# Small operations of a spectral block and gated MLP regrouped and moved between engines, on one core

## The chip, the core and the metric

The kernel runs on one core of a Trainium2 chip. A core has five engines that run side by side, each through its own list of instructions in order: TensorE (PE in the profile; PEld is its weight load) multiplies matrices, VectorE (DVE) and ScalarE (ACT) work element by element and read what TensorE leaves in PSUM, GpSimd (POOL) works element by element on SBUF, and SyncE (SP) issues the transfers between HBM and SBUF. An instruction waits on semaphores until what it reads is there, and everything behind it on its engine waits with it. The metric is the device time of one execution in microseconds (us), lower is better.

## What is computed

One token row set `x` of 8192 x 448 goes through two residual branches. `c` (448 numbers) gives six rows of 448 by `silu(c) @ w_mod`: shift, scale and gate of each branch.

```python
mod = (_silu(c) @ w_mod).reshape(c.shape[0], 6, 1, -1)
sa, ca, ga, sb, cb, gb = (mod[:, i] for i in range(6))
h = _layernorm(x) * (1 + ca) + sa
x = x + ga * irfft2(softshrink(block_mlp(rfft2(h))))      # 4 blocks of 112, complex, two layers
h = _layernorm(x) * (1 + cb) + sb
x = x + gb * ((gelu(h @ w_gate) * (h @ w_up)) @ w_down)   # 448 -> 1792 -> 448
```

The spelling of the spectral line is shortened here; the transform runs over the 8192 rows, the two layers of the MLP use complex 112 x 112 weights, and the shrink is by 0.01. All inputs and the output are float32.

## The kernel before

The program has three stages, written out engine by engine in the order of the source (`manual_schedule`), so the order of the source is the order of every engine's list.

**Stage one** (lines 130 to 330) reads `x` as 64 slices of 128 x 448 (`bb`, loaded four at a time as chunks `ch`), takes the mean and variance of each row, and multiplies each slice by the first Fourier factor `f1`, scaled by the rows' inverse deviation. A group of slices goes through a chain: VectorE takes statistics (`stats`, line 161) and joins them (`aggr_steps`), ScalarE takes a square root (line 188), VectorE makes the inverse and one correction step of Newton's method (lines 189 to 193, into `y`) and the scaled mean `nm`; then for each slice a scaled copy `fr` of `f1` is made (line 204 on ScalarE, line 206 on GpSimd), TensorE multiplies (`dft_a`, line 211), and ScalarE copies the result out of PSUM with the mean taken off (`out_a`, line 216). `means` (line 183) is one small matmul for each group. `store_t` writes finished chunks to `td` in HBM. The groups are `cuts` = 0, 2, 4, 8, 16, 24, 40, 56, 60, 64; a small planner (`ex`, `run`, with rough times `dve` and `pe`) sorts the calls and so interleaves the chain of one group with the statistics of the next. At its end two modulation rows (`mod_row0`, `mod_turn`, `mod_cols`) become columns.

**Stage two** works through 32 units. `step(i)` (line 534) issues, in this order: the loads of unit i + 2 (`fetch_t`), the hooks "load" and "pe", `stage_s2` of unit i, `split_t` of unit i + 1 (its low half `tl` on GpSimd), the hook "act", `stage_m2` of unit i - 2 with the split of its result (`yl` on GpSimd, twice), `stage_i1` of unit i - 3, the hook "dve", `stage_m1` of unit i - 1. The hooks, filled by `at(i, hook, ...)`, carry preparation for stage three: loads and norms of the gate and up weights (`load_w`, `squares`, `norms`: steps 1 to 16), sums of the down weights (`down_sums`), and the modulation rows. `load_mod_row` loads 4 x 112 rows of `w_mod`, and `mod_row` makes one modulation row on all partitions with 16 weight-and-matmul passes (8 matmuls of 128 x 224, line 637). Small operations on scales are put into a list `tiny` (by `VL` and `GL`, which record an operation for VectorE or GpSimd) and issued one by one between the larger ones by `drip()`. `all_max` (line 680) takes a maximum over partitions: TensorE turns a column (`turn`), VectorE reduces it, and TensorE spreads it again (`spread`) into the same PSUM bank of tag "pd", which `stage_i1` also uses; a tag has two banks.

**Stage three** (line 900 on) is the second branch: gate, up and down products over 32 row groups of 256.

Of the kernel before, what the change touches and what calls it, by code (L numbers as in the profile page):

```python
# [10 lines left out]
F32 = mybir.dt.float32  # L11
# [34 lines left out]
def spectral_geglu(ctx, tc, x, wt_in, wgu, wd, cvec, wmod, cf1, cs2, cmi, cgm, out):  # L46
# [88 lines left out]
    with ExitStack() as actx:  # L135
# [41 lines left out]
        def scale_steps(bs):  # L177

            g = slice(bs[0], bs[-1] + 1)

            def means():
                ps = bank("pc", "psmu")
                T.matmul(ps[:, : len(bs)], f1, nm[:, g], start=True, stop=True)
                S.copy(mu[:, g], ps[:, : len(bs)])


            return [
                lambda: S.activation(q[:, g], mv[:, g, 1], AF.Sqrt, bias=eps),
                lambda: V.reciprocal(q[:, g], q[:, g]),
                lambda: V.tensor_tensor(t[:, g], q[:, g], q[:, g], ALU.mult),  # L190
                lambda: V.scalar_tensor_tensor(t[:, g], mv[:, g, 1], EPS, t[:, g], op0=ALU.add, op1=ALU.mult),
                lambda: V.scalar_tensor_tensor(t[:, g], t[:, g], -0.5, q[:, g], op0=ALU.mult, op1=ALU.mult),
                lambda: V.scalar_tensor_tensor(y[:, g], q[:, g], 1.5, t[:, g], op0=ALU.mult, op1=ALU.add),
                lambda: V.scalar_tensor_tensor(nm[:, g], mv[:, g, 0], -0.5 if len(bs) >= 8 else -1.0, y[:, g], op0=ALU.mult, op1=ALU.mult),
                means,
            ]
# [3 lines left out]
        def scaled(bb):  # L200

            f = ap.tile([128, 128], F32, tag="fr", name="fr", bufs=6)
            if bb < 8 or bb % 4 == 3:
                S.activation(f, f1, AF.Copy, scale=y[:, bb : bb + 1])
            else:
                G.tensor_scalar(f, f1, y[:, bb : bb + 1], None, op0=ALU.mult)
            frs[bb] = f
# [82 lines left out]
        for g, bs in enumerate(groups + [[]]):  # L290
            done = None
            if pend:
                aggr, sqrt, rest, mean = pend
                run(aggr)
                ex(dve, sqrt)
                ready = dve + 0.6
            for bb in bs:
                if pend and not done and dve >= ready:
                    run(rest)
                    done = dve  # L300
                ex(dve, stats, bb)
# [32 lines left out]
    with ExitStack() as bctx:  # L334
# [260 lines left out]
        for z in zh + hh_:  # L595
            V.tensor_copy(z[96:113, 0], ones[96:113])
        mod_turn()
        mod_cols()
        split_t(*units[0], el=V)
        bp = bctx.enter_context(tc.tile_pool(name="bp", bufs=1, side="right"))  # L600
# [21 lines left out]
        def load_mod_row(pool, q):  # L622
            out = []
            for hh in range(2):
                if pool is None:
                    wm = bp1.tile([128, GB, HC], F32, tag="tr", name="tr", bufs=2)[:112]
                else:
                    wm = raw_tile(pool)[:112, :, :HC]
                dma(wm, wmod[q][:, :, hh * HC : (hh + 1) * HC])
                out.append(wm)  # L630
            return out

        def mod_row(key, dst=None):
            ps = bank("pd", "psm")
            for hh, wm in enumerate(raws.pop(key)):
                for k in range(4):
                    T.matmul(ps[:, hh * HC : (hh + 1) * HC], cs[:, k : k + 1].to_broadcast([112, 128]), wm[:, k, :], start=k == 0, stop=k == 3)
            if dst is None:
                return ps[:, :D]
            S.copy(dst, ps[:, :D])  # L640

        def row_scales():

            VL.tensor_scalar(cb_r, cb_r, 1.0, None, op0=ALU.add)
# [3 lines left out]
            VL.scalar_tensor_tensor(bnd, rmax[:, 0:1], 21.2, rmax[:, 1:2], op0=ALU.mult, op1=ALU.add)  # L648
            VL.tensor_scalar(bnd, bnd, 1.01, 1e-30, op0=ALU.mult, op1=ALU.add)
            pow2(sk, bnd)  # L650
            VL.tensor_scalar(sb_r, sb_r, sk, None, op0=ALU.mult)
            VL.tensor_scalar(cb_r, cb_r, sk, None, op0=ALU.mult)

# [25 lines left out]
        def all_max(dst, src, n, first=(), then=()):  # L679
# [12 lines left out]
            def spread():  # L692
                T.matmul(at_[0][:, 128 : 128 + n], onesr[:n], dia, start=True, stop=True)

            VL.tensor_copy(col, src)
            tiny.extend(first or [free] * 3)
            tiny.append(turn)
            tiny.append(lambda: V.tensor_reduce(top, at_[0][:n, :128], mybir.AxisListType.X, ALU.max))
            VL.tensor_scalar(dia, identb[:n, :n], top, None, op0=ALU.mult)
            tiny.extend(then or [free] * 3)  # L700
            tiny.append(spread)
            tiny.append(lambda: V.tensor_copy(dst, at_[0][:, 128 : 128 + n]))

# [4 lines left out]
        def scales1():  # L708
# [9 lines left out]
            first = [  # L718
                lambda: V.tensor_tensor(hb2, rmax[:, 0:1], rmax[:, 1:2], ALU.add),
                lambda: V.tensor_tensor(hb2, hb2, hb2, ALU.mult),  # L720
                lambda: V.tensor_scalar(hb2, hb2, 1.02 * D, 1e-30, op0=ALU.mult, op1=ALU.add),
            ]

            then = [
                lambda: V.tensor_tensor(mx2, nrm[:, 0], nrm[:, 1], ALU.mult),
                lambda: V.tensor_scalar(mx2, mx2, hb2, None, op0=ALU.mult),
                lambda: V.tensor_tensor(sa_act, mx2[:, :NP], mx2[:, NP:], ALU.max),
# [3 lines left out]
        def scales2():  # L731
            pow2(sw, mxa)
            inv_pow2(dsw, sw)
            inv_pow2(hs, sk)
            VL.tensor_scalar(dsw, dsw, hs, None, op0=ALU.mult)
            VL.tensor_copy(dg, dsw[:, 0:1])
            pow2(sa_act, sa_act, 13)
            inv_pow2(isa, sa_act)
            VL.tensor_scalar(sa_act, sa_act, dsw[:, 1:2], None, op0=ALU.mult)

        def down_scales():

            VL.tensor_tensor(dsc, dn, isa, ALU.mult)
            VL.tensor_reduce(hs, dsc, mybir.AxisListType.X, ALU.max)
# [155 lines left out]
    with ExitStack() as cctx:  # L900
# [417 lines left out]
```

## Time and profile before

| what | value |
| --- | --- |
| time, median of 3 runs (lowest to highest) | 1981.11 us (1980.15 to 1984.56) |
| the profiled execution: its time, its span | 1981.5 us, 1979.7 us |
| mean granted TensorE clock | 0.99 |
| VectorE, ScalarE, GpSimd busy | 58%, 39%, 60% of the span |
| stage one; stage two; stage three | about 0 to 84; 84 to 410; 410 to 1980 us |

The page lists busy times by engine; the timeline of one engine gives start, duration, line, operation, output <- inputs, and in brackets how long the engine was idle before and what released it. A float32 matmul counts as two or more passes, so a count such as x4 stands for two matmuls of 448 columns. The windows view gives, for each stretch, the busy time of PE, PEld, DVE, ACT and POOL with their counts, the mean granted TensorE clock, the busy share of the transfer engines and GB/s.

### The profile page before, as it was taken

The page shows a single profiled execution, that of the slowest core. Times are in us where ns is not written, and L with a number is a line of the kernel's source. Part 1 is how long each engine was busy: PE and PEld are TensorE (multiplying, and loading weights), DVE is VectorE, ACT ScalarE, POOL GpSimd, SP SyncE. Part 2 cuts the span into 40 slices and gives each one's busy share as a digit, 9 for nine tenths or more (in the row PEclk, how much of TensorE's full clock was granted, in tenths as well). Part 3 has the DMA queues.
Part 4 walks back from the last instruction along what each step waited for, and adds up shares of the span by engine and source line. Part 5 has one row for each costly group of instructions (what it writes and reads, how often), then busy time and mean ns, then how long its engine had stood idle before and what let it go on. Part 6 is the DMA issues. An engine that isn't in the chain of part 4 may idle for free.

```text
span 1979.7 us, 43432 instructions
## 1 busy us (share of the span) xinstructions
PE 1922.4 (97%) x17674; PEld 1710.8 (86%) x17674; DVE 1141.2 (58%) x2355; ACT 767.7 (39%) x1290; POOL 1184.7 (60%) x1479
## 2 busy tenths in 40 slices
PE   6899989988999999999999999999999999999998
PEld 3598989977888888888888888889888888989898
DVE  7478889866555554555555555555555555555533
ACT  5665658643333333333333333333333333333322
POOL 2355646536666666666666666666666666666644
PEclk9899989999999999999999999999999999999999
DMA  9797757641111111111111111111111111111000
GB/s 347 265 284 248 228 147 221 169 149 45 56 43 43 45 49 46 43 42 43 43 42 45 49 42 43 43 42 42 43 43 43 43 43 44 43 42 44 22 16 20
DMA packets 150539, 165.75 MB, mean 84 GB/s; under 512 B 83953, under 2 KB 125169, under 8 KB 149954
## 3 DMA queue, kind: packets, MB, share of 16 engines
q1 hardware_dynamic: 150338, 162.97, 27.2%
q8 instruction: 138, 2.26, 0.5%
q14 instruction: 63, 0.52, 0.1%
HBM read 97.49 MB, written 49.66 MB: 74 GB/s over the span
## 4 chain that ended last, share of the span: by engine, by line
PE 85%; DVE 10%; ACT 3%; issue 1%; DMA 1%; POOL 1%; SPq 0%; ACTq 0%; DVEq 0%; POOLq 0%
PE pgu L1033 52%; PE pdn L1101 7%; PE pdn L1099 7%; PE pdn L1100 7%; DVE y L469 3%; PE ps L211 2%; DVE zl L384 1%; DVE t L461 1%; DVE hl L439 1%; PE pi L933 1%; DVE st L161 1%; PE pi L931 1%; PE pi L932 1%; PE ps L375 0%; DVE wd L868 0%
## 5 line engine op out<-in xcount | busy, mean ns | idle before, releaser
L1033 PE MATMUL pgu<-nt,wh 128*128 128x256 f16 x6272 | 833.0, 273 | 1.8 <-DVE nt L1024 1.8
L1033 PEld LDWEIGHTS <-wh 128*128 128x128 f16 x6272 | 601.9, 98 | 99.2 <-issue 32.2
L1069 ACT ACTIVATE gel<-pgu,dg 128x256 f32<-128x256 f32 x448 | 200.4, 473 | 797.8 <-PE pgu L1033 762.8
L1033 PE MATMUL pgu<-nt,wl 128*128 128x256 f16 (+1 forms) x3584 | 500.7, 272 | 0.0
L1099 PE MATMUL pdn<-wd,ac 128*128 128x224 f16 x1568 | 407.0, 260 | 2.0 <-ACT p L1128 2.0
L1101 PE MATMUL pdn<-wd,ac 128*128 128x224 f16 x1568 | 406.9, 260 | 0.2 <-DVE ac L1092 0.2
L1100 PE MATMUL pdn<-wd,ac 128*128 128x224 f16 x1568 | 406.9, 260 | 0.0
L1080 POOL TENSOR_TENSOR x<-x 128x128 f32<-128x128 f32 x223 | 242.3, 1087 | 234.2 <-DVE x L1074 234.2
L1092 DVE SCALAR_TENSOR_TENSOR ac<-x,sa_act,ac 128x896 f16<-128x896 f32 (+1 forms) x225 | 308.2, 1370 | 83.6 <-ACT ac L1091 83.6
L1033 PEld LDWEIGHTS <-wl 128*128 128x128 f16 (+1 forms) x3584 | 297.6, 97 | 56.6 <-issue 23.6
L1074 DVE TENSOR_TENSOR x<-pgu,gel 128x256 f32<-128x256 f32 x448 | 179.6, 418 | 284.4 <-ACT gel L1069 283.7
L1091 ACT ACTIVATE ac<-x,sa_act 128x896 f16<-128x896 f32 (+1 forms) x225 | 232.9, 1035 | 48.8 <-POOL x L1083 46.7
L1134 POOL TENSOR_TENSOR o<-u,p 128x224 f32<-128x224 f32 x32 | 21.1, 658 | 294.3 <-DVE u L1133 294.3
L1081 POOL TENSOR_TENSOR x<-x 128x128 f32<-128x128 f32 x223 | 159.9, 717 | 17.5
L1100 PEld LDWEIGHTS <-ac 128*128 128x128 f16 x1568 | 153.8, 98 | 2.7 <-issue 2.1
L1099 PEld LDWEIGHTS <-ac 128*128 128x128 f16 x1568 | 153.7, 98 | 0.8 <-issue 0.2
L1101 PEld LDWEIGHTS <-ac 128*128 128x128 f16 x1568 | 153.7, 98 | 0.7 <-DVE ac L1092 0.5
L106 POOL TENSOR_TENSOR yl<-y,yh 128x448 fp32r<-128x448 f32 x63 | 77.8, 1235 | 90.9 <-ACT yh L104 82.9
L1082 POOL TENSOR_TENSOR x<-x 128x128 f32<-128x128 f32 x223 | 114.7, 515 | 0.0
L1083 POOL TENSOR_TENSOR x<-x 128x128 f32<-128x128 f32 x223 | 107.6, 482 | 0.0
L469 DVE TENSOR_TENSOR y<-pm,t 64x224 f32<-64x224 f32 x256 | 99.5, 389 | 8.2
L106 POOL TENSOR_TENSOR tl<-tr,th 128x896 f16<-128x896 f32 x30 | 57.4, 1914 | 67.6 <-ACT th L104 64.8
(288 smaller groups left out, 2794.9 us busy)
## 6 DMA issues: line engine op xcount, KB each, us to landing
tr<-td SPq DMA_DIRECT2D x64, 224.0 KB, 4.3
raw<-in_gu SPq DMA_DIRECT2D x28, 512.0 KB, 5.9
vd<-us SPq DMA_DIRECT2D x64, 224.0 KB, 3.0
xx<-in_x SPq DMA_DIRECT2D x32, 448.0 KB, 3.2
v<-vd SPq DMA_DIRECT2D x64, 224.0 KB, 2.7
out<-x SPq DMA_DIRECT2D x31, 448.0 KB, 2.6
nt<-pk SPq DMA_TRANSPOSE x480, 2.3
tb<-in_x SPq DMA_DIRECT2D x8, 896.0 KB, 17.5
```

The source lines that it names most:

```text
L106: (el or V).tensor_tensor(lo, src, h, ALU.subtract)
L469: V.tensor_tensor(y[ri * 64 : ri * 64 + 64, gi], pv[si, ri], tv[si, ri], ALU.subtract)
L1033: T.matmul(pgu[i, t, q][:, pr * H : (pr + 1) * H], w[rows, tw, f0 : f0 + 128], nts[i][rows, tn, :], start=start, stop=stop, skip_group_che ...
L1069: S.activation(gl, ps[:, :H], AF.Gelu_apprx_tanh, scale=dg)
L1074: V.tensor_tensor(dst, ps[:, H : 2 * H].rearrange("p (b c) -> p b c", b=2), gl.rearrange("p (b c) -> p b c", b=2), ALU.mult)
L1080: e.tensor_tensor(s1, a21, a22, ALU.add)
L1081: e.tensor_tensor(s2, s1, a11, ALU.subtract)
L1091: S.activation(ac[:, 0, k], x[:, k], AF.Copy, scale=sc)
L1092: V.scalar_tensor_tensor(ac[:, 1, k], x[:, k], sc, ac[:, 0, k], op0=ALU.mult, op1=ALU.subtract)
L1099: T.matmul(ps, ac[:, 0, ka], wds[t][:, 0, kb], start=t == 0, stop=False)
L1100: T.matmul(ps, ac[:, 0, ka], wds[t][:, 1, kb], start=False, stop=False)
L1101: T.matmul(ps, ac[:, 1, ka], wds[t][:, 0, kb], start=False, stop=t == NP - 1)
```

## The change

1. Stage one: groups of at most eight slices, the Newton step written with one operation less, and the scaled copies `fr` of slices 0 to 3 on VectorE and of 4 to 7 on GpSimd instead of ScalarE. The planner waits for two statistics (`ready`), not one, between square root and inverse in the later groups.
2. Modulation rows: all four rows of stage three are loaded in stage two (steps 1, 3, 5, 8). GpSimd multiplies the four tiles of a row by the columns of `cs` and adds them up in place (`mod_sum`, one step later, hook "dve"), and TensorE sums the 112 partitions with one matmul by ones (`mod_row`, at the head of the step after that, hook "pe").
3. `row_scales` moves from step 9 to step 6, and many small operations of the scales move from VectorE to GpSimd.
4. `all_max` takes a bank for `turn` and another for `spread`.
5. `gb_r` is scaled on GpSimd in step 24, and the first `split_t` stands ahead of `mod_turn`.

```diff
-        cuts = [0, 2, 4, 8, 16, 24, 40, 56, 60, 64]
+        cuts = [0, 2, 4, 8, 16, 24, 32, 40, 48, 56, 60, 64]
...
-                lambda: V.tensor_tensor(t[:, g], q[:, g], q[:, g], ALU.mult),
-                lambda: V.scalar_tensor_tensor(t[:, g], mv[:, g, 1], EPS, t[:, g], op0=ALU.add, op1=ALU.mult),
+                lambda: V.scalar_tensor_tensor(t[:, g], mv[:, g, 1], EPS, q[:, g], op0=ALU.add, op1=ALU.mult),
...
-            if bb < 8 or bb % 4 == 3:
+            if bb >= 8 and bb % 4 == 3:
                 S.activation(f, f1, AF.Copy, scale=y[:, bb : bb + 1])
             else:
-                G.tensor_scalar(f, f1, y[:, bb : bb + 1], None, op0=ALU.mult)
+                (V if bb < 4 else G).tensor_scalar(f, f1, y[:, bb : bb + 1], None, op0=ALU.mult)
...
-                ready = dve + 0.6
+                ready = dve + (0.6 if g < 3 else 1.2)
...
+        def mod_sum(key):
+            r = raws[key]
+            G.tensor_scalar(r[0], r[0], cs[:, 0:1], None, op0=ALU.mult)
+            for k in range(1, 4):
+                G.tensor_scalar(r[k], r[k], cs[:, k : k + 1], None, op0=ALU.mult)
+                G.tensor_tensor(r[0], r[0], r[k], ALU.add)
+
+        def mod_row(key, dst):
             ps = bank("pd", "psm")
-            for hh, wm in enumerate(raws.pop(key)):
-                for k in range(4):
-                    T.matmul(ps[:, hh * HC : (hh + 1) * HC], cs[:, k : k + 1].to_broadcast([112, 128]), wm[:, k, :], start=k == 0, stop=k == 3)
+            T.matmul(ps[:, :D], onec.to_broadcast([112, 128]), raws.pop(key)[0], start=True, stop=True)
             S.copy(dst, ps[:, :D])
...
             def spread():
-                T.matmul(at_[0][:, 128 : 128 + n], onesr[:n], dia, start=True, stop=True)
+                at_[1] = bank("pd", "pmx")
+                T.matmul(at_[1][:, :n], onesr[:n], dia, start=True, stop=True)
...
-            VL.tensor_scalar(dia, identb[:n, :n], top, None, op0=ALU.mult)
+            GL.tensor_scalar(dia, identb[:n, :n], top, None, op0=ALU.mult)
...
-        at(3, "load", pre, npool, "cb", load_mod_row, 4)
-        at(5, "load", pre, npool, "sb", load_mod_row, 3)
-        at(6, "pe", mod_row, "cb", cb_r)
-        at(8, "pe", mod_row, "sb", sb_r)
+        for n, (key, q, dst) in zip((1, 3, 5, 8), (("cb", 4, cb_r), ("sb", 3, sb_r), ("ga", 2, ga_r), ("gb", 5, gb_r))):
+            at(n, "load", pre, npool, key, load_mod_row, q)
+            at(n + 1, "dve", mod_sum, key)
+            at(n + 2, "pe", mod_row, key, dst)
...
-        at(9, "dve", row_scales)
+        at(6, "dve", row_scales)
...
-        at(31, "load", pre, None, "ga", load_mod_row, 2)
-        at(32, "load", pre, fp, "gb", load_mod_row, 5)
+        at(24, "dve", lambda: G.tensor_scalar(gb_r, gb_r, ds_d, None, op0=ALU.mult))
...
-        mod_row("ga", ga_r)
...
-        gb = mod_row("gb")
...
-        S.copy(gb_r, gb)
...
-        V.tensor_scalar(gb_r, gb_r, ds_d, None, op0=ALU.mult)
```

Where the order of instructions changes, at three places. First GpSimd's list in steps 1 to 3 of stage two (`tl` and `yl` are low halves of float32 values, `raw` the tiles of the row "cb"). Before:

```order
L106 TENSOR_TENSOR tl_929<-tr_814,th_928 128x896
L106 TENSOR_TENSOR yl_955<-y_949,yh_954 128x448
L106 TENSOR_TENSOR yl_979<-y_973,yh_978 128x448
L106 TENSOR_TENSOR tl_1067<-tr_890,th_1066 128x896
L106 TENSOR_TENSOR yl_1093<-y_1087,yh_1092 128x448
```

And of the changed kernel:

```order
L108 TENSOR_TENSOR tl_954<-tr_835,th_953 128x896
L108 TENSOR_TENSOR yl_980<-y_974,yh_979 128x448
L108 TENSOR_TENSOR yl_1004<-y_998,yh_1003 128x448
L633 TENSOR_SCALAR raw_839<-raw_839,cs_79 112x448
L635 TENSOR_SCALAR raw_839<-raw_839,cs_79 112x448
L636 TENSOR_TENSOR raw_839<-raw_839 112x448
L635 TENSOR_SCALAR raw_841<-raw_841,cs_79 112x448
L636 TENSOR_TENSOR raw_839<-raw_839,raw_841 112x448
L635 TENSOR_SCALAR raw_841<-raw_841,cs_79 112x448
L636 TENSOR_TENSOR raw_839<-raw_839,raw_841 112x448
L108 TENSOR_TENSOR tl_1102<-tr_915,th_1101 128x896
```

Seven operations, four products by a column and three additions, now stand between the second `yl` of step 2 and the `tl` of step 3.

Second TensorE's list where step 3 begins (`pm1` is the last matmul of step 2, `pw` the norms). Before:

```order
L425 MATMUL pm1_998<-zl_849,w1h_93 112x256
L426 MATMUL pm1_998<-zh3_735,w1l_94 112x256
L670 LDWEIGHTS sq_932
L670 MATMUL pw_1024<-onesb_73,sq_932 128x1
L670 MATMUL pw_1024<-onesb_73,sq_932 128x1
```

And of the changed kernel:

```order
L426 MATMUL pm1_1030<-zl_874,w1h_95 112x256
L427 MATMUL pm1_1030<-zh3_756,w1l_96 112x256
L640 MATMUL psm_1056<-raw_839,onec_80 128x448
L672 LDWEIGHTS sq_957
L672 MATMUL pw_1059<-onesb_73,sq_957 128x1
```

The matmul that reads the sum `raw_839` is the first of step 3; the same is found at the heads of steps 5, 7 and 10, and the eight matmuls of 128 x 224 for each row, which stood at the heads of steps 6 and 8 and twice between stages two and three, are gone.

Third VectorE's list of stage one around slice 24. Before, a chain of sixteen:

```order
L161 BN_STATS st_132<-xt_129 128x6 x3
L161 BN_STATS st_132<-xt_130 128x6 x4
L161 BN_STATS st_132<-tb 128x6 x8
L170 TENSOR_TENSOR t<-st_132 128x16
L171 TENSOR_TENSOR mv<-st_132 128x16
L189 RECIPROCAL q<-q 128x16
```

And of the changed kernel, two chains of eight:

```order
L163 BN_STATS st_134<-xt_131 128x6 x2
L163 BN_STATS st_134<-xt_132 128x6 x4
L172 TENSOR_TENSOR t<-st_134 128x8
L173 TENSOR_TENSOR mv<-st_134 128x8
L163 BN_STATS st_134<-tb 128x6 x2
L191 RECIPROCAL q<-q 128x8
L163 BN_STATS st_134<-tb 128x6 x6
```

The inverse for slices 24 to 31 now comes after two statistics of the next eight, not after those of sixteen slices.

More of the change, by code (lines that the diff above doesn't have):

```diff
@@ L75, in spectral_geglu @@
     cs = cpool.tile([112, 4], F32, name="cs")
+    onec = cpool.tile([112, 1], F32, name="onec")
+    V.memset(onec, 1.0)
     nrm = cpool.tile([128, 2, NFT], F32, name="nrm")
@@ L189, in scale_steps @@
                 lambda: V.reciprocal(q[:, g], q[:, g]),
-                lambda: V.tensor_tensor(t[:, g], q[:, g], q[:, g], ALU.mult),
-                lambda: V.scalar_tensor_tensor(t[:, g], mv[:, g, 1], EPS, t[:, g], op0=ALU.add, op1=ALU.mult),
+                lambda: V.scalar_tensor_tensor(t[:, g], mv[:, g, 1], EPS, q[:, g], op0=ALU.add, op1=ALU.mult),
                 lambda: V.scalar_tensor_tensor(t[:, g], t[:, g], -0.5, q[:, g], op0=ALU.mult, op1=ALU.mult),
-                lambda: V.scalar_tensor_tensor(y[:, g], q[:, g], 1.5, t[:, g], op0=ALU.mult, op1=ALU.add),
+                lambda: V.scalar_tensor_tensor(y[:, g], t[:, g], 1.5, q[:, g], op0=ALU.add, op1=ALU.mult),
                 lambda: V.scalar_tensor_tensor(nm[:, g], mv[:, g, 0], -0.5 if len(bs) >= 8 else -1.0, y[:, g], op0=ALU.mult, op1=ALU.mult),
@@ L596, in spectral_geglu @@
             V.tensor_copy(z[96:113, 0], ones[96:113])
+        split_t(*units[0], el=V)
         mod_turn()
         mod_cols()
-        split_t(*units[0], el=V)
         bp = bctx.enter_context(tc.tile_pool(name="bp", bufs=1, side="right"))
@@ L623, in load_mod_row @@
             out = []
[L624 to L630, printed above, removed]
-            return out
-        def mod_row(key, dst=None):
-            ps = bank("pd", "psm")
-            for hh, wm in enumerate(raws.pop(key)):
-                for k in range(4):
-                    T.matmul(ps[:, hh * HC : (hh + 1) * HC], cs[:, k : k + 1].to_broadcast([112, 128]), wm[:, k, :], start=k == 0, stop=k == 3)
-            if dst is None:
-                return ps[:, :D]
+            for i in range(2):
+                wm = raw_tile(pool).rearrange("p q c -> p (q c)")[:112, : 2 * D].rearrange("p (q c) -> p q c", q=2)
+                dma(wm, wmod[q][:, 2 * i : 2 * i + 2])
+                out += [wm[:, 0], wm[:, 1]]
+            return out
+        def mod_sum(key):
[5 more added lines that the diff above has]
+        def mod_row(key, dst):
+            ps = bank("pd", "psm")
+            T.matmul(ps[:, :D], onec.to_broadcast([112, 128]), raws.pop(key)[0], start=True, stop=True)
             S.copy(dst, ps[:, :D])
         def row_scales():
-            VL.tensor_scalar(cb_r, cb_r, 1.0, None, op0=ALU.add)
+            GL.tensor_scalar(cb_r, cb_r, 1.0, None, op0=ALU.add)
             for j, r in enumerate((cb_r, sb_r)):
@@ L647, in row_scales @@
             bnd = cpool.tile([128, 1], F32, name="hb")
-            VL.scalar_tensor_tensor(bnd, rmax[:, 0:1], 21.2, rmax[:, 1:2], op0=ALU.mult, op1=ALU.add)
-            VL.tensor_scalar(bnd, bnd, 1.01, 1e-30, op0=ALU.mult, op1=ALU.add)
+            GL.tensor_scalar(bnd, rmax[:, 0:1], 21.2, None, op0=ALU.mult)
+            GL.tensor_tensor(bnd, bnd, rmax[:, 1:2], ALU.add)
+            GL.tensor_scalar(bnd, bnd, 1.01, 1e-30, op0=ALU.mult, op1=ALU.add)
             pow2(sk, bnd)
-            VL.tensor_scalar(sb_r, sb_r, sk, None, op0=ALU.mult)
-            VL.tensor_scalar(cb_r, cb_r, sk, None, op0=ALU.mult)
+            GL.tensor_scalar(sb_r, sb_r, sk, None, op0=ALU.mult)
+            GL.tensor_scalar(cb_r, cb_r, sk, None, op0=ALU.mult)
         def load_w(pool, pr, j):
@@ L692, in spread @@
             def spread():
-                T.matmul(at_[0][:, 128 : 128 + n], onesr[:n], dia, start=True, stop=True)
-            VL.tensor_copy(col, src)
+                at_[1] = bank("pd", "pmx")
+                T.matmul(at_[1][:, :n], onesr[:n], dia, start=True, stop=True)
+            GL.tensor_copy(col, src)
             tiny.extend(first or [free] * 3)
@@ L698, in all_max @@
             tiny.append(lambda: V.tensor_reduce(top, at_[0][:n, :128], mybir.AxisListType.X, ALU.max))
-            VL.tensor_scalar(dia, identb[:n, :n], top, None, op0=ALU.mult)
+            GL.tensor_scalar(dia, identb[:n, :n], top, None, op0=ALU.mult)
             tiny.extend(then or [free] * 3)
             tiny.append(spread)
-            tiny.append(lambda: V.tensor_copy(dst, at_[0][:, 128 : 128 + n]))
+            tiny.append(lambda: V.tensor_copy(dst, at_[1][:, :n]))
         mxa = cpool.tile([128, 2], F32, name="mxa")
@@ L718, in scales1 @@
             first = [
-                lambda: V.tensor_tensor(hb2, rmax[:, 0:1], rmax[:, 1:2], ALU.add),
-                lambda: V.tensor_tensor(hb2, hb2, hb2, ALU.mult),
-                lambda: V.tensor_scalar(hb2, hb2, 1.02 * D, 1e-30, op0=ALU.mult, op1=ALU.add),
+                lambda: G.tensor_tensor(hb2, rmax[:, 0:1], rmax[:, 1:2], ALU.add),
+                lambda: G.tensor_tensor(hb2, hb2, hb2, ALU.mult),
+                lambda: G.tensor_scalar(hb2, hb2, 1.02 * D, 1e-30, op0=ALU.mult, op1=ALU.add),
             ]
             then = [
-                lambda: V.tensor_tensor(mx2, nrm[:, 0], nrm[:, 1], ALU.mult),
-                lambda: V.tensor_scalar(mx2, mx2, hb2, None, op0=ALU.mult),
+                lambda: G.tensor_tensor(mx2, nrm[:, 0], nrm[:, 1], ALU.mult),
+                lambda: G.tensor_scalar(mx2, mx2, hb2, None, op0=ALU.mult),
                 lambda: V.tensor_tensor(sa_act, mx2[:, :NP], mx2[:, NP:], ALU.max),
@@ L734, in scales2 @@
             inv_pow2(hs, sk)
-            VL.tensor_scalar(dsw, dsw, hs, None, op0=ALU.mult)
-            VL.tensor_copy(dg, dsw[:, 0:1])
+            GL.tensor_scalar(dsw, dsw, hs, None, op0=ALU.mult)
+            GL.tensor_copy(dg, dsw[:, 0:1])
             pow2(sa_act, sa_act, 13)
             inv_pow2(isa, sa_act)
-            VL.tensor_scalar(sa_act, sa_act, dsw[:, 1:2], None, op0=ALU.mult)
+            GL.tensor_scalar(sa_act, sa_act, dsw[:, 1:2], None, op0=ALU.mult)
         def down_scales():
-            VL.tensor_tensor(dsc, dn, isa, ALU.mult)
+            GL.tensor_tensor(dsc, dn, isa, ALU.mult)
             VL.tensor_reduce(hs, dsc, mybir.AxisListType.X, ALU.max)
@@ L750, in down_scales2 @@
             pow2(hs, ds_d, 13)
-            VL.tensor_scalar(dsc, isa, hs, None, op0=ALU.mult)
+            GL.tensor_scalar(dsc, isa, hs, None, op0=ALU.mult)
             inv_pow2(ds_d, hs)
```

## The prediction

> **What bounds the kernel now.** I read the engines' shares first, then the busy time by stretches (start:end, length, then busy and count of PE, PEld, DVE, ACT, POOL; granted clock, DMA share, GB/s), then the rows in order of time.
>
> ```profile
> PE 1922.4 (97%) x17674; PEld 1710.8 (86%) x17674; DVE 1141.2 (58%) x2355; ACT 767.7 (39%) x1290; POOL 1184.7 (60%) x1479
> 65.00:68.00 3.00, 3.00 (x9) 1.51 (x9) 2.97 (x8) 2.62 (x6) 3.00 (x3) 1.00 1.01 423
> 104.20:113.30 9.10, 9.03 (x88) 8.60 (x86) 7.47 (x17) 6.06 (x11) 4.30 (x4) 1.00 0.82 240
> 122.10:130.80 8.70, 8.70 (x88) 8.53 (x87) 7.50 (x16) 6.06 (x11) 4.21 (x3) 1.00 1.01 279
> 174.40:187.80 13.40, 10.69 (x99) 9.69 (x98) 13.04 (x31) 7.47 (x16) 5.50 (x5) 1.00 0.61 187
> 242.70:260.10 17.40, 12.00 (x80) 10.81 (x80) 13.02 (x28) 6.64 (x12) 6.05 (x5) 0.80 0.48 129
> 277.20:291.00 13.80, 10.79 (x82) 9.71 (x80) 10.71 (x23) 7.69 (x13) 8.61 (x6) 0.88 0.63 168
> 291.00:299.30 8.30, 8.30 (x80) 8.18 (x80) 6.85 (x18) 6.41 (x10) 3.08 (x2) 1.00 0.39 109
> ```
>
> TensorE is the bound. Row three is step 3 of stage two and row four step 5: PE full, GpSimd half idle. The places where PE isn't full are step 10 (174.40), step 17 (242.70) and step 20 (277.20), where VectorE's list of small scale operations is late, and gaps in stage one. The change touches all of these. My sums are made on the profiled execution, 1981.5 us (its span 1979.7 and 1.8 around it); the median of the runs shown, 1981.11, is the same within 0.4 us.
>
> **The sums on GpSimd.** PE takes its list in order, and the matmul that reads the sum of a row is now the first of steps 3, 5, 7 and 10, ahead of the norms `pw`. GpSimd can begin the seven operations only after the second `yl` of the step before, and these end late:
>
> ```profile
> 104.20 0.60 PE L670 MATMUL pw<-onesb,sq 128*128 128x1 bf16 x8
> 105.42 1.14 POOL L106 TENSOR_TENSOR yl<-y,yh 128x448 fp32r<-128x448 f32 x1 [1.13 <-ACT yh L104]
> 122.08 0.60 PE L670 MATMUL pw<-onesb,sq 128*128 128x1 bf16 x8
> 122.28 1.14 POOL L106 TENSOR_TENSOR yl<-y,yh 128x448 fp32r<-128x448 f32 x1 [1.20 <-ACT yh L104]
> 142.61 0.60 PE L670 MATMUL pw<-onesb,sq 128*128 128x1 bf16 x8
> 142.81 1.14 POOL L106 TENSOR_TENSOR yl<-y,yh 128x448 fp32r<-128x448 f32 x1 [1.20 <-ACT yh L104]
> 173.00 0.60 PE L670 MATMUL pw<-onesb,sq 128*128 128x1 bf16 x8
> 174.13 1.14 POOL L106 TENSOR_TENSOR yl<-y,yh 128x448 fp32r<-128x448 f32 x1 [1.21 <-ACT yh L104]
> ```
>
> When PE arrives at step 3 (104.20), that `yl` still has until 106.56: 2.36 us. The other three pairs give 1.34, 1.34 and 2.27; together 7.3. Then come four products by a column and three additions, each on the result of the one before or two before:
>
> ```profile
> 24.66 3.52 POOL L206 TENSOR_SCALAR fr<-f,y 128x128 f32<-128x128 f32 x6 [22.75 <-DMA tb<-in_x]
> L1113 POOL TENSOR_TENSOR o<-o,gb_r 128x448 f32<-128x448 f32 x62 | 70.3, 1133 | 2.4
> 132.14 0.66 POOL L783 TENSOR_TENSOR m<-m 128x224 f32<-128x224 f32 x1
> 132.88 0.66 POOL L784 TENSOR_TENSOR m<-m 128x224 f32<-128x224 f32 x1
> ```
>
> An addition of 448 columns costs 1.1 us (1133 ns). Dependent ones start 0.74 apart for 0.66 of work, so 0.08 per hand-over, about 0.45 for six. The trace has no product by a column over 448 columns on GpSimd; it has one over 128, at 3.52/6 = 0.59. It cannot be less than 0.59, and 3.5 times that, 2.05, if all of it grows with length. Between them I take 1.4: the `m` and `o` additions grow by 0.47 for 224 more columns, so 0.59 grows by 0.67 for 320 more to 1.26 at their rate, and a little more since the product was slower than an addition to begin with. One sum is then 4 x 1.4 + 3 x 1.1 + 0.45 = 9.3 us (6.1 to 12.0). While it runs everything behind the matmul waits: the norms, the tokens' spectra, the mixing; and ScalarE and VectorE wait for those. PE had no free time in these steps, so the wait is lost: 7.3 + 4 x 9.3 = **+44.5** (31.7 to 55.3).
>
> After a wait the clock is low. The row at 41.69 below shows it: four matmuls took 3.30 after an idle of 3.62, and 1.77 at 25.32. That is 1.55 after a short idle; step 17 had a mean clock of 0.80 over 17.4 us, which is up to 3.5 lost. Four times 2.0: **+8** (6 to 14).
>
> The matmuls themselves:
>
> ```profile
> 130.82 3.19 PE L637 MATMUL psm<-raw,cs 112*128 112x224 f32 x16
> 405.69 3.19 PE L637 MATMUL psm<-tr,cs 112*128 112x224 f32 x16
> 410.12 0.66 ACT L104 CAST vh<-v 128x224 fp32r<-128x224 f32 x2 [0.67 <-DMA vd<-us]
> 414.92 5.92 PE L637 MATMUL psm<-raw,cs 112*128 112x224 f32 x16
> 421.46 0.56 PE L1015 MATMUL ptr<-ident,pk 128*128 128x128 f16 x7 [0.57 <-ACT pk L988]
> ```
>
> Sixteen pieces (0.19 each) held PE 3.0 us in steps 6 and 8. A row of 448 columns is now four pieces, 0.76. The rows "ga" and "gb" stood at 405.69 and 414.92, where PE would have waited anyway: for the transfer behind `vh` (410.12) and for ScalarE's `pk` (421.46). So 4 x 0.76 - 2 x 3.0 = **-3**. With "gb" gone, PE is idle for some 6 us ahead of 421.46 and starts stage three cold: **+2** (0 to 3).
>
> **Stage one.**
>
> ```profile
> 21.20 1.75 PE L211 MATMUL ps<-xt,fr 128*128 128x448 f32 x4
> 23.14 0.31 ACT L188 ACTIVATE q<-mv,eps 128x8 f32<-128x8 f32 x1
> 24.60 3.77 DVE L161 BATCH_NORM_STATS2 st<-xt 128x6 f32<-128x448 f32 x7
> 25.32 1.77 PE L211 MATMUL ps<-xt,fr 128*128 128x448 f32 x4 [2.37 <-POOL fr L206]
> 30.63 3.78 DVE L161 BATCH_NORM_STATS2 st<-xt 128x6 f32<-128x448 f32 x7
> 41.69 3.30 PE L211 MATMUL ps<-xt,fr 128*128 128x448 f32 x4 [3.62 <-POOL fr L206]
> 57.21 12.27 PE L211 MATMUL ps<-tb,fr 128*128 128x448 f32 x32
> 74.37 6.17 PE L228 MATMUL psm<-wm,cs 112*1 112x448 f32 x16
> ```
>
> A slice costs PE 0.757 (the second group spans 30.63 - 24.60 = 6.03 on VectorE). With groups of eight PE has 8 x 0.757 + 0.14 = 6.2 per group and VectorE 6.0, minus 0.2 for the operation dropped, 5.8: the next `fr` are ready before PE wants them, and the idle of 3.62 with its cold 1.55 at 41.69 goes. The start at 25.32 comes about 0.8 sooner, at 24.5: then 56 x 0.757 + 7 x 0.14 = 43.4 ends at 67.9, where stage one ended at 74.37: **-6.4** (-7 to 0, if a chain is late in each group). What is late next is the input: the DMA share is 1.01 until 68, and three stores of 0.22 MB go behind it, some 1.6 us, so 1 or 2 us of the gain may go there.
>
> **The scales and the rest.** Step 17 took 17.4 us and step 20 13.8, while step 21 (291.00) took 8.3.
>
> ```profile
> PE pi L498 <- ACT us L501: 2.3, 1, 2.3
> PE pi L498 <- ACT us L501: 1.9, 1, 1.9
> 178.54 1.11 DVE L514 SCALAR_TENSOR_TENSOR hb<-rmax 128x1 f32<-128x1 f32 x1
> 177.72 1.91 POOL L106 TENSOR_TENSOR tl<-tr,th 128x896 f16<-128x896 f32 x1 [2.46 <-ACT th L104]
> 248.94 1.65 DVE L514 TENSOR_SCALAR mxd<-identb,mxt 2x2 bf16<-2x2 bf16 x1
> ```
>
> Of their 14.6 surplus, PE's wait for the shared bank (first row: step 17; second row: step 20; us, times, longest) goes with the two banks. Small VectorE operations that took 1.1 to 1.65 while GpSimd worked go to GpSimd itself; the reductions stay and still queue. I take a bit more than half: **-8** (-3 to -14.6). `row_scales` moves from step 9 to step 6, behind a wait of PE: the surplus of step 10, 13.4 - 10.7 = 2.7 of PE idle, goes: **-2.7** (0 to -4).
>
> At nothing: the `memset`; the same bytes of "ga" and "gb" loaded 25 steps earlier (PE and not a queue ends those steps; if it did not, 1.6 MB would cost 4 us at 423 GB/s); `split_t` ahead of `mod_turn` (VectorE and PE wait there for `cs` anyway; else its operation, 1.9 by the `tl` row of the same size); the product `gb_r` by `ds_d` on GpSimd in step 24 (idle half of a step; else 1.4). Sum: 44.5 + 8 - 3 + 2 - 6.4 - 8 - 2.7 = +34.4, of 1981.5: **2015 us**, slower.
>
> [...]
>
> **The rivals.** *Cheap sums.* The product costs 0.6 for 448 columns as for 128: a sum is 4 x 0.6 + 3.3 + 0.45 = 6.1, the four 12.8 less: 2002. For it: 0.59 may be mostly a fixed cost. Against: the additions grow with length. *Dear sums.* 2.05 each: 10.6 more, 2026. *Stage one stays broken.* A group of eight waits for its chain as one of sixteen did; 6.4 more: 2022. For it: each hand-over between VectorE, ScalarE and GpSimd costs a fraction of a us and there are more of them now.
> *The wait is absorbed: faster.* In steps 3 to 9 PE's rows look full, but DMA shares are 0.82 and 1.01; if the transfers set the pace, matmuls that look busy are only spread out, a pause at a step's head is caught up later in it, and only the gains are left: 1981.5 - 3 + 2 - 6.4 - 8 - 2.7 = 1963. It decides only if a sum and its `yl` (1.3 to 2.4) fit in what a step can give back; to break even, with gains of 18.1, each wait may cost 18.1/4 = 4.5 in all, so a sum may take 2.7. Three additions alone take 3.3, and the clock in these rows is 1.00 with weight loads at 8.5 of 8.7, so I give it little.
>
> **How the numbers follow.** Forecast 0.50 (2008 to 2022), cheap sums 0.18, dear sums 0.14, stage one broken 0.09, absorbed 0.06, partly absorbed so that nothing can be told 0.03. A measurement of this kernel can tell about 0.2%, 4 us. Faster 0.06, same 0.03, slower 0.91. The range takes in the cheap sums with full gains in the scales (2002 - 6.6, and 5 more from the lower ends of clock and stage one: 1990) and the dear ones with small gains (2026 + 5 and the higher clock cost, 6, and 3 left over: 2040).
>
> **What would show it.** Four idle gaps of PE of 10 to 12 us ahead of `psm`, ended by GpSimd's `raw` in steps 3, 5, 7 and 10, and a lower clock behind each; products on GpSimd near 1.4 us; matmuls without a gap from 25 to 68; steps 17 and 20 nearer to 10 than to 15. It is wrong if PE's gaps there are under 5 us, if the matmul's operand is ready before PE comes, or if the steps with a gap are no longer in all than before.

## The result and the profile after

The changed kernel takes 2015.9 us (2014.7 to 2016.9), the kernel before 1981.0: 1.0172 times as long, 95% interval 1.0155 to 1.0190, or 35 us more. The runs below give this ratio and, in brackets, its interval in the same way. The profiled execution has a span of 2013.8, 34.1 more than the 1979.7 of before.

First the shares of the engines in the profile after; then TensorE's four largest waits, from its rows in order of time (start, us, engine, line, operation; in brackets how long it had waited and for whom).

```profile
PE 1914.2 (95%) x17622; PEld 1700.3 (84%) x17622; DVE 1136.5 (56%) x2351; ACT 764.7 (38%) x1286; POOL 1232.5 (61%) x1532
```

```profile
111.17 1.11 PE L640 MATMUL psm<-raw,onec 112*128 112x448 f32 x1 [11.38 <-POOL raw L636]
143.12 1.11 PE L640 MATMUL psm<-raw,onec 112*128 112x448 f32 x1 [10.40 <-POOL raw L636]
174.49 1.11 PE L640 MATMUL psm<-raw,onec 112*128 112x448 f32 x1 [10.40 <-POOL raw L636]
216.42 1.11 PE L640 MATMUL psm<-raw,onec 112*128 112x448 f32 x1 [11.32 <-POOL raw L636]
```

TensorE has 8 us less work and the kernel is 34 us longer: PE's share falls from 97% to 95%. The four waits, one for each row of the modulation, sum to 43.5 us, at the heads of steps 3, 5, 7 and 10. What ends them are GpSimd's operations on the tile `raw`, shown by the view of that tile (line, operation, count: shortest/median/longest ns, first and last start):

```profile
L635 POOL TENSOR_SCALAR raw<-raw,cs x12: 1404/1406/1409, 103.3 to 213.8; 112x448 f32<-112x448 f32 x12
L636 POOL TENSOR_TENSOR raw<-raw x12: 1127/1127/1127, 104.8 to 215.2; 112x448 f32<-112x448 f32 x12
L633 POOL TENSOR_SCALAR raw<-raw,cs x4: 1405/1407/1411, 101.9 to 207.2; 112x448 f32<-112x448 f32 x4
```

A product of a tile by a column takes 1.41 us, an addition of two tiles 1.13. The busy time by stretches (columns as before) shows the wait of step 3 and what follows it:

```profile
99.50:110.90 11.40, 0.29 (x3) 0.07 (x1) 1.92 (x4) 1.63 (x4) 10.96 (x9) 0.71 0.88 249
110.90:123.50 12.60, 12.33 (x86) 11.17 (x87) 6.03 (x13) 5.36 (x9) 3.27 (x3) 0.72 0.00 0
123.50:132.40 8.90, 8.90 (x89) 8.66 (x88) 7.05 (x15) 6.17 (x11) 4.20 (x3) 1.00 0.93 294
```

In the wait hardly anything but GpSimd works. In the stretch behind it, which holds the matmul of the sum and step 3, PE is busy nearly throughout and yet needs 12.6 us, at a granted clock of 0.72; the step after that runs at 1.00 and takes 8.9. And stage one, where the two matmuls (x4 in passes) at 41.69 had come after a wait of 3.62 and a slow start:

```profile
41.69 1.77 PE L212 MATMUL ps<-tb,fr 128*128 128x448 f32 x4
67.28 6.17 PE L229 MATMUL psm<-wm,cs 112*1 112x448 f32 x16
79.06 0.94 ACT L106 CAST th<-tr 128x896 f16<-128x896 f32 x1 [5.04 <-DMA tr<-td]
```

No wait stands there now, and the matmuls of `wm` that end stage one begin at 67.28, 7.1 us before their start of 74.37. But `th`, which the first spectra need, then waits for the transfer of `tr`, 5.0 us.

Where the time went, by PE's rows at the same places in both traces (after minus before, in us):

| stretch | change |
|---|---|
| to the end of stage one | -7.1 |
| from there to the head of step 3 | +2.5 |
| the four waits | +43.5 |
| matmuls of the rows, and the clock in the steps behind the waits, to step 10 (net) | +6.1 |
| surplus of steps 10 and 11 | -4.3 |
| steps 17 to 21 | -8.8 |
| step 22 to the end, with the start of stage three | +2.1 |
| sum, before rounding | +34.1 |

### The profile page after: what moved, and what is told of

Read it like the earlier page. It is cut to its first block, busy times and chain, and to the rows that moved or that the text cites. A ratio compares the mean times of both kernels' runs of the same rounds, so it can differ in the third digit from the quotient of the medians.

```text
span 2013.8 us, 43386 instructions
## 1 busy us (share of the span) xinstructions
PE 1914.2 (95%) x17622; PEld 1700.3 (84%) x17622; DVE 1136.5 (56%) x2351; ACT 764.7 (38%) x1286; POOL 1232.5 (61%) x1532
## 4 chain that ended last, share of the span: by engine, by line
PE 82%; DVE 7%; POOL 4%; DMA 2%; ACT 2%; issue 1%; SPq 0%; DVEq 0%; ACTq 0%; POOLq 0%
PE pgu L1034 50%; PE pdn L1102 7%; PE pdn L1100 7%; PE pdn L1101 7%; DVE y L470 2%; PE ps L212 1%; DMA td<-xt 1%; POOL raw L635 1%; PE pi L934 1%; DVE t L462 1%; DVE zl L385 1%; POOL raw L636 1%; PE pi L932 1%; DVE hl L440 1%; PE pi L933 1%
## 5 line engine op out<-in xcount | busy, mean ns | idle before, releaser
L1075 DVE TENSOR_TENSOR x<-pgu,gel 128x256 f32<-128x256 f32 x448 | 179.6, 418 | 285.0 <-ACT gel L1070 284.4
```

The lines of the kernel that those rows point to most:

```text
L1075: V.tensor_tensor(dst, ps[:, H : 2 * H].rearrange("p (b c) -> p b c", b=2), gl.rearrange("p (b c) -> p b c", b=2), ALU.mult)
```

## Experiments

Each was timed against the kernel before on the same chip, and its ratio to it is given.

**1. The matmul one step later.**

```
-            at(n + 2, "pe", mod_row, key, dst)
+            at(n + 3, "pe", mod_row, key, dst)
```

> The changed kernel with the four psm matmuls one step later (steps 4, 6, 8, 11), everything else as it is. Theory (TensorE waits in order for GpSimd's sum): the sum ends 11.4 us after the head of step n+2, a step without a wait lasts 8.8, so only some 2.6 us of wait are left at the head of step n+3, and up to 1 us more for the tl that stands behind the sum on GpSimd: 3 to 4 in place of 10.4 to 11.4, and a clock that falls less. 2015.9 - 4 x 7.5 - 4 x 2 = 1978 (1970 to 1992). Rival (what costs is GpSimd's added work, 9.2 us a row, wherever it is waited for, since tl and yl come late): it stays within 5 of 2015.

It takes 1982.8 us, 1.0008 (0.9999 to 1.0017): 33 us of the loss go by moving four matmuls. GpSimd is busy for as long as in the changed kernel (1232 us in both), so its work as such isn't what costs. It is 5 us above the value expected, though inside the range. Its waits: 2.40 and 1.72 for the first two rows, then one of a kind that the theory had not listed. Rows of GpSimd, VectorE and PE in step 7 of this kernel:

```profile
153.44 1.34 POOL L515 TENSOR_SCALAR cb_r<-cb_r 128x448 f32<-128x448 f32 x1
154.81 0.62 DVE L515 TENSOR_REDUCE rmax<-cb_r 128x1 f32<-128x448 f32 x1 [10.05 <-POOL cb_r L515]
155.35 0.15 DVE L679 TENSOR_SCALAR nrm<-pw 128x2 f32<-128x2 f32 x1
155.55 0.74 PE L499 MATMUL pi<-yh,mih 128*128 128x448 f32 x1 [7.31 <-DVE nrm L679]
```

The addition of one to `cb_r`, which the change also gave to GpSimd, stands behind the sum of the next row. VectorE's `rmax` waits 10.05 for it, `nrm` stands behind `rmax`, and PE waits 7.31 for `nrm`, which must have read its bank (the matmuls of `pw` and `pi` share the two banks of the tag "pd"). The same kind of wait, three engines long. In the changed kernel this lies in the shadow of the wait of step 7.

**2. TensorE does the sums.**

```
-            T.matmul(ps[:, :D], onec.to_broadcast([112, 128]), raws.pop(key)[0], start=True, stop=True)
+            for k, wm in enumerate(raws.pop(key)):
+                T.matmul(ps[:, :D], cs[:, k : k + 1].to_broadcast([112, 128]), wm, start=k == 0, stop=k == 3)
...
-            at(n + 1, "dve", mod_sum, key)
```

> The changed kernel with the sums of the four rows by four matmuls of 448 columns each, at the same heads of steps 3, 5, 7 and 10, and nothing of them on GpSimd. Theory: the waits (43.5 in the trace of the changed kernel) and the low clock behind them (some 14 with the psm matmuls) go, four times 3.0 of matmuls come: 2015.9 - 43.5 - 14 + 12 = 1970 (1966 to 1975), and PE shows no idle over 2 us from step 1 to step 17. Rival (the four steps are held up by transfers anyway): over 1981.

It takes 1969.9, 0.9944 (0.9928 to 0.9960). Same places, same transfers, no sum to wait for: PE has no idle over 2 us from step 1 to step 16, and its largest wait there is 1.6. A row costs 3.0 us of matmuls (its step takes 11.8 in place of 8.8). So the transfers did not set the pace of these steps, and the rival in which the wait is absorbed falls.

**3 and 4. Stage one alone, the scales alone** (in the kernel before: the first all edits of stage one, the second the two banks and the small operations on GpSimd, with `row_scales` left in step 9).

> The kernel before with the edits of stage one alone (groups of eight, one operation less, the other engines of fr, split_t ahead of mod_turn). In the changed kernel stage one ends 7.1 us sooner, but the transfers behind it let only 4.7 through to step 3. Theory: 1981.0 - 4.7 = 1976.4 (1975 to 1978). Rivals: all of it counts, 1974; or the transfers take it back by step 9, 1981.

> The kernel before with the edits of the scales alone (two banks in the maximum over partitions, small operations of row_scales, scales and down_scales on GpSimd; row_scales stays in step 9). In the changed kernel steps 16 to 21 are 8.6 us shorter in all. Theory: 1981.0 - 8.6 = 1972.4 (1969 to 1974), the surplus of step 10 not much changed since row_scales stays. Rival (that gain came from the later state of the lists after the waits, or from row_scales in step 6): 1977 or more.

Stage one alone: 1976.7, 0.9975 (0.9964 to 0.9986), 4.2 us less; in the trace it is 4.8 us ahead of the kernel before in step 3, and 4.9 in the last step of stage two. The scales alone: 1971.6, 0.9947 (0.9926 to 0.9967), 9.3 less. Both are gains by themselves. Where the second comes from shows in step 17, in VectorE's and GpSimd's rows of this kernel:

```profile
244.23 0.27 DVE L700 TENSOR_REDUCE mxt<-pmx 2x1 f32<-2x128 f32 x1
244.59 0.29 POOL L514 TENSOR_SCALAR mxd<-identb,mxt 2x2 bf16<-2x2 bf16 x1 [1.26 <-DVE mxt L700]
244.88 1.90 POOL L106 TENSOR_TENSOR tl<-tr,th 128x896 f16<-128x896 f32 x1
```

On VectorE `mxd`, two by two numbers, had taken 1.65 at 248.94, until GpSimd's operation ended; on GpSimd it takes 0.29, ahead of `tl`.

**5, 10, 11 and 12. The parts of the scales.** First the bank alone:

```
-                T.matmul(at_[0][:, 128 : 128 + n], onesr[:n], dia, start=True, stop=True)
+                at_[1] = bank("pd", "pmx")
+                T.matmul(at_[1][:, :n], onesr[:n], dia, start=True, stop=True)
```

> The kernel before with one part of the scales' edits alone: spread takes a bank of its own, all operations stay on VectorE. Theory (the waits of 2.3 and 1.9 us for the shared bank in steps 17 and 20 go, and the rest of the 9.3 that all edits of the scales gave is VectorE's queue): 1981.0 - 4.2 = 1976.8 (1975 to 1978). Rivals: another wait takes their place, 1981; or the bank is all of it, 1971.6.

It takes 1976.7, 0.9981 (0.9972 to 0.9990): the number expected, though that is 3.4 less than the kernel before beside it, not 4.2. The places were wrong. The wait of step 17 is still there, in PE's rows of this kernel:

```profile
253.21 0.74 PE L498 MATMUL pi<-yh,mih 128*128 128x448 f32 x1 [2.32 <-ACT us L501]
```

ScalarE's copy `us` frees the bank, and it stands behind `yh`, which waits for VectorE's `y`: the late engine is VectorE, not the bank. Only the wait of step 20 went, with the slow matmuls behind it (the granted clock over that step was 0.88 in the kernel before). Step 11 is 1.6 shorter as well, with its wait of 1.3 still there, since the clock did not fall behind that wait in this execution (in the kernel before it was 0.85 over the 11.2 us of that step, which is 1.7 lost). So I ran the rest without the bank:

> The kernel before with the other part of the scales' edits alone: the small operations on GpSimd, but one bank as before. The run with two banks alone kept its wait of 2.3 in step 17 and lost that of 1.9 in step 20, with 1.1 to 1.4 in the step behind. Theory: the bank is worth about 3.4 and only in step 20, GpSimd's operations the rest, in steps 10, 11, 17 and 18: 1981.0 - 9.3 + 3.4 = 1975 (1973 to 1977), steps 10 to 18 as with all the edits, the wait of 1.9 in step 20 still there. Rival (either part alone frees most): 1972.

It takes 1970.0, 0.9949 (0.9936 to 0.9961), where 1975 was expected: as much as with the bank. Its wait in step 20 is there as foreseen:

```profile
275.67 0.47 PE L498 MATMUL pi<-yh,mih 128*128 128x448 f32 x1 [1.89 <-ACT us L501]
```

Both once more, side by side:

> All edits of the scales in the kernel before, once more, beside the next run on the same chip: apart they came out at 0.9947 and 0.9949 of the time before, though the trace of the one with its own bank is 3.2 us shorter. Theory (the bank is worth its wait in step 20, 3.2, also where GpSimd has the small operations, and the scatter of single runs, 1.5 us for each short wait that does or does not lower the clock, hid it): this one 2 to 4 us below the next. Rival (on top of the GpSimd operations the bank is worth nothing): within 1 us of it.

> The same without a bank of its own, beside the run above. Theory: 2 to 4 us above it, 1973. Rival: within 1 us of it.

1970.0 with the bank, 0.9950 (0.9938 to 0.9963), and 1971.4 without, 0.9953 (0.9940 to 0.9967): 1.4 apart, between theory and rival, and the intervals overlap. In both pairs of traces (runs 4 and 10, 11 and 12) step 20 is 2.1 us shorter with the bank; in the two steps behind, 0.4 is lost again, so some 1.7 remain. The small operations on GpSimd carry the gain; that the bank adds 1 to 2 us on top is likely by the traces and not shown by the times.

**6. TensorE works while it waits.**

```
+    V.memset(gb_r, 0.0)
...
             ps = bank("pd", "psm")
+            for _ in range(13):
+                T.matmul(ps[:, :D], cs[:, 0:1].to_broadcast([112, 128]), gb_r[:112], start=True, stop=True)
             T.matmul(ps[:, :D], onec.to_broadcast([112, 128]), raws.pop(key)[0], start=True, stop=True)
```

> The changed kernel with 13 more matmuls of 448 columns (9.9 us at full clock) ahead of each psm matmul, into the same bank, overwritten by it: TensorE works while it waits for the sum. The sum comes no sooner. Theory (the low clock behind a wait is a cost of its own, which the trace puts at 11 in all: 0.75 on each psm matmul and 1.3 to 2 in the step behind it): 2015.9 - 11 = 2005 (2002 to 2008). Rival (the steps behind the waits are slow for another reason, lists that fill again): 2016.

It takes 2009.6, 1.0148 (1.0133 to 1.0164): 6 us less than the changed kernel, by doing more, but less gain than expected. PE's rows in step 3:

```profile
100.86 9.93 PE L642 MATMUL psm<-gb_r,cs 112*128 112x448 f32 x26
112.43 1.02 PE L643 MATMUL psm<-raw,onec 112*128 112x448 f32 x2 [1.63 <-POOL raw L637]
```

The 13 added matmuls count as 26 passes. The sum comes no sooner; the step behind lasts 8.75 in place of 10.98. Over the four waits the trace gives 8.8 us, of which the time shows 6. I had said 11, with 2 us for step 10, which stays at 10.0 with this work ahead of it too, and in steps 3 and 10 the added work was some 1.6 us too short to reach the sum.

**7. No sum that is waited for.** The kernel before with stage one and scales as changed; the rows "cb" and "sb" are summed ahead.

```
+        for n in range(4):
+            at(2 + n, "dve", piece, "cb", V, n)
+        for n, ks in ((3, (0, 1)), (4, (2,)), (6, (3,))):
+            at(n, "dve", piece, "sb", G, *ks)
+        at(7, "pe", sum_row, "cb", cb_r)
+        at(8, "pe", sum_row, "sb", sb_r)
```

> The kernel before with the edits of stage one and of the scales, rows ga and gb and row_scales as before, and the rows cb and sb summed ahead in pieces of one step each: cb on VectorE (one operation a step in steps 2 to 5), sb on GpSimd (steps 3, 4 and 6), the psm matmuls in steps 7 and 8, so that no sum is waited for. Theory: 1981.0 - 4.2 - 9.3 (as measured apart) - 4.5 (sixteen pieces in steps 6 and 8 become two of 0.38 each, twice) = 1963 (1960 to 1966). Rival (a piece on a full VectorE or GpSimd delays what PE waits for): 1967 or more.

It takes 1962.9 (1962.1 to 1963.6), 0.9906 (0.9893 to 0.9920), faster than both kernels. GpSimd's products are no shorter (1407 ns); nobody waits for them. Stretches of its steps 3 and 5 to 7:

```profile
104.20:113.30 9.10, 9.10 (x89) 8.85 (x89) 8.58 (x18) 6.77 (x11) 6.27 (x6) 1.00 0.91 256
120.00:142.00 22.00, 22.00 (x204) 21.02 (x203) 19.17 (x40) 15.09 (x25) 16.89 (x16) 1.00 0.92 309
```

PE is full, VectorE and GpSimd fuller than before, the clock 1.00.

**8. The sums alone** (in the kernel before: the four rows loaded, summed and read as in the change, nothing else).

> The kernel before with the sums on GpSimd and their matmuls alone, as in the change; stage one, scales and row_scales in step 9 as before. Theory (the parts add up): 2015.9 + 4.2 + 9.3 = 2029 (2025 to 2033). Rival (the sums free VectorE's and PE's later lists too, or the waits hide part of the other stages): 2020 or less.

It takes 2031.0, 1.0248 (1.0234 to 1.0262), 51 us more than the kernel before beside it. With the gains of 4.2 and 9.3 measured apart that makes +37; the changed kernel has +35. The parts nearly add up.

**9. TensorE works ahead of stage three.**

```
         rsqrt0(0)
+        ps = bank("pd", "psm")
+        for _ in range(8):
+            T.matmul(ps[:, :HC], cs[:, 0:1].to_broadcast([112, 128]), gb_r[:112, :HC], start=True, stop=True)
```

> The changed kernel with eight matmuls of 224 columns (sixteen pieces, 3 us) where row gb stood before, behind the first inverse transforms of stage three; their result is read by nobody. Theory (without row gb TensorE idles 5.1 us there and starts stage three at a low clock, which costs 2.3 by the trace): 2015.9 - 2.3 = 2013.6, and the transposes ptr and the first pgu at full clock. Rival (ScalarE's pk is late for another reason): 2016, no row faster.

It takes 2015.4, 1.0176 (1.0162 to 1.0190): no difference that can be told, as the rival had it, but not for the rival's reason. In the trace stage three starts as the theory said, with a granted clock of 0.98 from 450 to 500 us where the changed kernel has 0.91; at 503 us PE is 2.0 ahead of the changed kernel (0.1 of it from before stage three), and at 627 it is 0.6 ahead. Between lies a wait of 2.0 that both have, and the window around it, first of the changed kernel, then of this one:

```profile
514.75 0.26 PE L1100 MATMUL pdn<-wd,ac 128*128 128x224 f16 x1 [2.00 <-ACT p L1129]
510.00:520.00 10.00, 8.01 (x84) 7.84 (x83) 4.72 (x12) 1.18 (x2) 2.46 (x4) 1.00 0.06 14
```

```profile
512.74 0.26 PE L1100 MATMUL pdn<-wd,ac 128*128 128x224 f16 x1 [2.01 <-ACT p L1129]
510.00:520.00 10.00, 7.99 (x67) 7.21 (x66) 2.82 (x7) 1.18 (x2) 2.80 (x4) 0.83 0.09 18
```

After the same wait the clock stayed at 1.00 in one and fell to 0.83 in the other, which took most of the gain (the last section shows what differs). The gain at the start is seen in the trace; in the time it isn't.

## Why the prediction was right

**The sums.** The order of PE's list, the place of the second `yl` and GpSimd's rate gave the waits: +44.5 predicted, 43.5 measured. The term that I had bounded from 0.59 to 2.05, the product of 448 columns, is 1.41; I had taken 1.4. The growth with length was the right guide, but the additions gave too little of it: 0.67 for 320 columns, where the product grew by 0.82 (0.59 to 1.41). What I added on top without a row made up for that. On VectorE the same product took 0.45 us (first operation on the row "cb" in run 7; in the kernel before, `sb_r` by `sk`, 128 x 448, took 0.45 at 185.52), so GpSimd is three times as slow here. Runs 1 and 2 show the wait as the cause: the same work on GpSimd with the reader one step later, or the same reader without the work, and the loss is gone.

**The clock**: +8 predicted; run 6 takes 8.8 away in the trace and 6 in the time. That the clock is low after a wait held for these four of 10.4 to 11.4 us (0.72, 0.76, 0.78 and 0.83 over the steps behind them), not for every short one (last section). The prediction's reading of the row at 41.69 is off by 0.02 (3.30 less 1.77 is 1.53), which changes nothing. **The matmuls**: -3 by 0.38 for a piece of 448 columns (12.27 for the 32 at 57.21). I wrote of four such pieces for a row; there are two, of 0.76 together, which is the price I had used.

**Stage one**: -6.4 predicted at its end, -7.1 measured. Two sizes inside it were off and partly cancel: the matmuls start at 22.8, not 24.5, and then take 44.5 to the row of `wm`, not 43.4 (the row at 57.21 gives 0.767 for a slice, not the 0.757 used). The "1 or 2" given back to the transfers, which the sum left out, is 2.5: 4.2 is left when stage one is alone. The transfers are busy to the last until 72 us now (before, half of 68 to 72), as the two traces show, the kernel before first:

```profile
68.00:72.00 4.00, 4.00 (x13) 2.13 (x13) 1.11 (x4) 2.36 (x6) 2.27 (x4) 1.00 0.52 215
```

```profile
68.00:72.00 4.00, 4.00 (x12) 0.92 (x11) 1.74 (x8) 1.62 (x4) 0.00 (x0) 1.00 1.01 407
```

That it is the transfers that hold `th` is read from its wait for `tr` and these shares; no run took bytes away.

**The scales**: -8 predicted, -8.8 in the changed kernel. The step that failed is the one on the bank: I put 2.3 and 1.9 us of PE's wait down to it, and run 5 shows that of step 17 unchanged with a bank of its own. VectorE's `y` was late there, and run 10 shows that the operations on GpSimd do nearly all. What I had named beside it, small operations on VectorE that took 1.11 to 1.65 us while GpSimd worked, was worth more than I gave it; that the sum of both came out at 8 is luck. One sign that I had named did not come: step 17 takes 13.5, nearer to 15 than to 10. Its wait for `us` is still 1.8 in the changed kernel, and the clock is 0.50 behind it, from 292.05 to 295.46; run 4 has the same wait without that fall, and 12.0. **Steps 10 and 11**: -2.7 predicted for `row_scales` in step 6; -4.3 measured, of which run 4 has 2.6 with `row_scales` still in step 9. So most of it isn't the move. About 1.0 of the 2.6 are shorter waits and the rest a fall of the clock in step 11 (to 0.85 over the step in the kernel before) that is missing; it is missing in run 5 too, where all operations stay on VectorE, so that the operations on GpSimd took it away is not shown.

**The start of stage three**: +2 predicted, +2.1 in the trace after; run 9 shows the cause at its place, and no difference in the time.

**The total.** That 2015.9 met the sum (1981.5 + 34.4) to a fraction of a us is luck: stage one gained nearly 2 less than its term, steps 10 and 11 and the scales 2.4 more, and the waits and the clock were off by about 1 each. The mechanism, and the order of the terms, is what the runs bear out.

Of the rivals, cheap sums fall by the 1.41 of the product, dear ones too; stage one came out continuous; and the faster case, the wait absorbed by a step that transfers hold up, falls by run 2 and by the steps behind the waits, which took 10 to 11 us where 8.8 would have done, never less.

## What to carry to other kernels

An operation moved from a full engine to a half idle one was cheap here only where nobody waited for it (run 1 moved nothing but the readers: 1982.8 us in place of 2015.9). So look up who reads the result, where that reader stands in its in-order list, and when the new engine can begin, which here was after its own late work. Nine us of work on GpSimd, begun late, cost some thirteen at the head of a step; the same kind of work in pieces a few steps ahead cost nothing that shows. And a change of several parts is worth taking apart: two of three here were gains that the third hid.

## What the runs showed of the hardware

- **Two tiny VectorE operations lasted until GpSimd's ended.** In the kernel before, `mxd` ran on VectorE from 248.94 for 1.65 us while `tl` ran on GpSimd from 248.68 for 1.89; they end together, at 250.6. `hb` from 178.54 for 1.11 beside a `tl` from 177.72 for 1.91 is the same: both end at 179.6. `mxd` takes 0.20 in step 20 with GpSimd idle (there it is a single number), and 0.29 on GpSimd. No run here looks behind this.
- **Whether a wait of 2.0 us was followed by a lower clock went with where it fell.** In step 27 PE waits 2.7 us for `hl` in every kernel. Two executions of one program (runs 4 and 11), windows around it:

```profile
333.82 0.37 PE L450 MATMUL pm<-w2h,hl 112*128 112x224 f32 x1 [2.72 <-DVE hl L439]
330.00:342.00 12.00, 9.28 (x94) 8.98 (x93) 10.46 (x17) 7.88 (x14) 5.58 (x4) 1.00 0.58 159
```

```profile
334.45 0.55 PE L450 MATMUL pm<-w2h,hl 112*128 112x224 f32 x1 [2.75 <-DVE hl L439]
330.00:342.00 12.00, 9.25 (x63) 8.87 (x62) 10.64 (x16) 7.12 (x12) 4.76 (x3) 0.72 0.52 144
```

Clock 1.00 and the step 11.2 long, or 0.72 and 14.0. The record of the granted clock in the traces shows what differs. In all fourteen profiled executions it is either 1.00 or 0.50, and the stretches of 0.50 within one execution begin whole multiples of 3.41 us apart and, but for the one at the program's end, last one to seven times 3.41 us. In the kernel before the first five begin at 41.38, 85.76, 188.16, 253.01 and 287.14, the last four of them 13, 43, 62 and 72 times 3.413 us after the first. So one can draw periods of 3.41 us and look how a wait lies in them. Here are two periods around the wait of 2.0 of run 9, then two around the same wait in the changed kernel:

```profile
510.37:513.78 3.41, 1.40 (x15) 1.24 (x14) 1.37 (x3) 1.18 (x2) 1.26 (x3) 1.00 0.03 9
513.78:517.19 3.41, 3.41 (x21) 2.79 (x20) 0.39 (x1) 0.00 (x0) 1.00 (x1) 0.50 0.13 25
```

```profile
510.50:513.91 3.41, 2.25 (x24) 2.10 (x22) 3.21 (x7) 0.39 (x1) 0.00 (x0) 1.00 0.00 0
513.91:517.33 3.42, 2.58 (x27) 2.58 (x27) 0.37 (x1) 0.79 (x2) 2.27 (x3) 1.00 0.11 24
```

In run 9 the wait (510.73 to 512.74) lies within one period, and the next one has half the clock. In the changed kernel (512.75 to 514.75) the border at 513.91 cuts it in two, and the clock stays. Over the fourteen executions this wait lies within one period in four (the kernel before and runs 7, 9 and 10), and those are the four with 0.50 behind it; in the kernel before it is the wait from 478.85 to 480.83, in the period from 478.28 to 481.70, and the clock is 0.50 from there to 485.11. The wait of step 27 is cut into 1.82 and 0.90 in run 4, and into 1.91 and 0.84 in run 11. How much idle time in a period it takes is not shown; other gaps fall in the same periods. As the periods lie differently in each execution (a border is at 510.37 in run 9 and at 510.50 in the changed kernel), this may be why single executions of one kernel scatter by up to 7 us (run 4: 1966.8 to 1973.9), and why a gain of 2 us seen in a trace can be missing from a median; that is my reading, and no run tests it.
